# Output stage by seven block products, and an earlier attention schedule

## The chip, the cores and the metric

The kernel runs on one core of one Trainium2 chip. The time is the device time of one execution in microseconds (us). TensorE is the matmul engine, VectorE (DVE in the profile), ScalarE (ACT) and GpSimd (POOL) work element by element, and SyncE (SP) only issues DMAs. PSUM is where TensorE writes: eight banks of 512 fp32 numbers in each of 128 partitions. GpSimd doesn't read it here; it works on SBUF.

## The reference

Eight batches of 576 tokens with 8 heads of 64 go through a linear attention, and its output goes through a feed-forward network without a nonlinearity behind its product:

```python
q_p = phi(q, cos_w, sin_w)          # relu(q)*cos next to relu(q)*sin, 128 features
k_p = phi(k, cos_w, sin_w)
kv = np.einsum('bhsf,bhsd->bhfd', k_p, v)
z = np.sum(k_p, axis=2)
num = np.einsum('bhsf,bhfd->bhsd', q_p, kv)
den = np.einsum('bhsf,bhf->bhs', q_p, z)[..., None] + 1e-06
x = (num / den) laid out as [4608, 512]
a = x @ w1                          # [512, 1024]
b = x @ w2
out = ((a * b) @ w3) @ w_out        # w3 [1024, 1024], w_out [1024, 512]
```

## The kernel before

TensorE multiplies in bf16 and sums in fp32. The kernel first forms `w34b` = w3 @ w_out (1024 x 512) while tile 0 is at work, so that the network is two stages for each of nine tiles of 512 tokens:

- *Products*: for each of eight chunks `jc` of 128 hidden columns, four matmuls with w1 (`aT`) and four with w2 (`bT`), 512 wide (L432). ScalarE copies `aT` to `asb` (L469), VectorE multiplies `asb` with `bT` in PSUM to `abT[:, jc, :]` (L473).
- *Output*: for each of four blocks of 128 tokens, eight matmuls of `abT` with `w34b`, 512 wide (L486). ScalarE copies the sum to `osb` (L493). GpSimd issues the stores for tiles 0 to 7, two for a tile, at planned steps (L611); the last tile's go from SyncE, the last half block's from SyncE and ScalarE (L505).

The four PSUM tiles of these stages come from `ffn_tile` (L421): two pools of two buffers, so every tile reuses the bank of the fourth tile before it, and its first matmul waits for that tile's last reader. Two more banks hold `pnum`, a single buffer for attention, and two hold transposes.

`ffn_groups` is a generator. Each `yield` ends a step: a tile has 24, sixteen for the products (two for a `jc`) and eight for the output; tile 0 has 40. Tile t from 1 on begins at step 16+24t, so tile 2 at 64, tile 3 at 88, tile 8 at 208. All engines execute in the order in which the program emits their instructions; nothing is reordered. Between two steps the calls stand that `at(step, ...)` put there. Thus attention is woven into the feed-forward work:

- `plan_loads` issues the loads of k, v and q of a batch from GpSimd, each behind `hold_back` (L516): a one-element copy by ScalarE (`mark`) that GpSimd copies on (`seen`), so that the DMA is not issued before ScalarE has come so far.
- `prep_k` and `prep_q` make the features of one of five chunks: half by VectorE (L259), half by ScalarE (L263). From the fourth chunk of batch 1 on, queries are transposed by a DMA from SyncE (L277). `prep_v` copies values, from batch 2 on by GpSimd (L283).
- `kv_chunk` adds a chunk to the key-value products, eight 65-wide matmuls into `pnum` (L291). Behind the fifth, ScalarE and then VectorE copy them to `kvs` (L296, L297).
- `num` multiplies a chunk's queries with `kvs`, eight 65-wide matmuls into `pnum` (L349), and VectorE normalizes: three instructions, L359 to L361, to `xblk`.
- `x_tr` brings `xblk` into `xT`, the tile's input: in batches 0 and 1 by TensorE and a copy (L389), later by a DMA transpose from SyncE (L383).

`plan` gives the steps of these calls for a batch: `kf`, `qf` and `vc` for the features, `kv`, `nu` for `num`, `xt` for `x_tr` (as `nu` if left out). Batches 4 to 7 take theirs from `bases` (L598): a batch's first `num` is at its base.

Of the kernel before, what the change touches and what calls it, by code (L numbers as in the profile page):

```python
# [10 lines left out]
FP32 = mybir.dt.float32  # L11
BF16 = mybir.dt.bfloat16
I32 = mybir.dt.int32
ALU = mybir.AluOpType
ACTF = mybir.ActivationFunctionType

P = 128
# [51 lines left out]
def kernel(  # L69
# [11 lines left out]
    nc = tc.nc  # L81
# [4 lines left out]
    NT = T // 512  # L86

    const = ctx.enter_context(tc.tile_pool(name="const", bufs=1))
# [282 lines left out]
    def x_tr(b, c, by_vector=False):  # L371
        R, rows = ROWS[c], out_rows(b, c)
        xblk = att[b]["x"].pop(c)
        xf = xblk[:].rearrange("p g h d -> p (g h d)")
        if b % 2 == 0:
            slot = S * b + 128 * c
        else:
            slot = S * b + (0 if c == 4 else 64 + 128 * c)
        t, o = divmod(slot, 512)
        if t not in xT:  # L380
            xT[t] = xtp.tile([P, 4, 512], BF16, name="xT")
        if b >= 2 or (b == 1 and c == 3):
            nc.sync.dma_start_transpose(out=xT[t][:, :, ds(o, R)], in_=xf[rows])  # L383
            return
        pst = ps_tr.tile([P, 8, 128], BF16, name="pst")
        for kc in range(4):
            nc.tensor.transpose(pst[:, kc, :], xf[:, ts(kc, 128)], identb[:])
        copy = nc.vector.tensor_copy if by_vector else nc.scalar.copy
        copy(out=xT[t][:, :, ds(o, R)], in_=pst[:, 0:4, rows])  # L389
# [11 lines left out]
    def store(eng, osb, g, n, cols=slice(0, DM)):  # L401
# [13 lines left out]
        for i, rows in enumerate(parts):  # L415
            on = eng[i % 2] if isinstance(eng, tuple) else eng
            on.dma_start(out=rows[:, :, cols], in_=osb[64 * i:64 * i + rows.shape[0], :, cols])  # L417

    ffn_tiles = [0]

    def ffn_tile():  # L421
        pool = ps_ffn[ffn_tiles[0] // 2 % 2]
        ffn_tiles[0] += 1
        return pool.tile([P, 512], FP32, name="ffnps")

    def ffn_groups(t):
        x = xT[t]
        abT = fsb.tile([P, 8, 512], BF16, name="abT", bufs=2)

        def products(out, w, jc, tok):  # L430
            for kc in range(4):
                nc.tensor.matmul(out, lhsT=w[:, kc, ts(jc, 128)], rhs=x[:, kc, tok],  # L432
                                 start=(kc == 0), stop=(kc == 3))

        def on_half(half):

            for pair in range(2):
                a, b = ffn_tile(), ffn_tile()
                if pair == 0 and t == 0:
                    for quarter in range(2):  # L440
                        for i in range(2):
                            for ps, w in ((a, w1b), (b, w2b)):
                                products(ps[:, ds(256 * i + 128 * quarter, 128)], w, i,
                                         ds(256 * half + 128 * quarter, 128))
                            if half == 0 and quarter == 0 and i == 0:
                                yield
                        if quarter == 0:
                            yield
                else:
                    for ps, w in ((a, w1b), (b, w2b)):  # L450
                        for i in range(2):
                            products(ps[:, ts(i, 256)], w, 2 * pair + i, ts(half, 256))
                        if w is w1b and (t == 1 or half == 0):
                            yield
                asb = fsb.tile([P, 512], BF16, name="asb")
                nc.scalar.copy(out=asb[:], in_=a[:, :])
                nc.vector.tensor_mul(out=abT[:, ts(pair, 2), ts(half, 256)],
                                     in0=asb[:].rearrange("p (i n) -> p i n", i=2),
                                     in1=b[:, :].rearrange("p (i n) -> p i n", i=2))
                yield  # L460

        if t < 2:
            yield from on_half(0)
            yield from on_half(1)
        for jc in range(4 if t < 2 else 0, 8):
            aT = ffn_tile()
            products(aT[:, :], w1b, jc, slice(0, 512))
            asb = fsb.tile([P, 512], BF16, name="asb")
            nc.scalar.copy(out=asb[:], in_=aT[:, :])  # L469
            yield  # L470
            bT = ffn_tile()
            products(bT[:, :], w2b, jc, slice(0, 512))
            nc.vector.tensor_mul(out=abT[:, jc, :], in0=asb[:], in1=bT[:, :])  # L473
            yield
        if t == 0:
            for jp in range(8):
                for part in range(2):
                    w34_mm(jp, part)
                    yield
            early.close()  # L480
            holds.append(ctx.enter_context(tc.tile_pool(name="hold", bufs=HELD,
                                                        reuse_waits="tile")))
        for ms in range(3 if t == NT - 1 else 4):
            ops = ffn_tile()
            for jc in range(8):
                nc.tensor.matmul(ops[:, :], lhsT=abT[:, jc, ts(ms, 128)], rhs=w34b[:, jc, :],  # L486
                                 start=(jc == 0), stop=(jc == 7))
                if jc == 3:
                    yield
            if ms % 2 == 0:  # L490
                osb = holds[0].tile([P, 2, 512], FP32, name="osb")
                kept.append(osb)
            nc.scalar.copy(out=osb[:, ms % 2, :], in_=ops[:, :])  # L493
            if t == NT - 1:
                store(nc.sync, osb[:, ms % 2:ms % 2 + 1, :], 4 * t + ms, 1)
            yield
        if t == NT - 1:
            for half in range(2):
                cols = ts(half, 256)
                ops = ffn_tile()  # L500
                for jc in range(8):
                    nc.tensor.matmul(ops[:, 0:256], lhsT=abT[:, jc, ts(3, 128)],
                                     rhs=w34b[:, jc, cols], start=(jc == 0), stop=(jc == 7))
                nc.scalar.copy(out=osb[:, 1, cols], in_=ops[:, 0:256])
                store((nc.sync, nc.scalar), osb[:, 1:2, :], 4 * t + 3, 1, cols)  # L505
                yield


    HELD = 10
    holds, kept = [], []  # L510
    slots = [[] for _ in range(40 + 24 * (NT - 1))]

    def at(s, *calls):
        slots[s] += calls
# [8 lines left out]
    def plan(b, kf, vc, kv, qf, nu, loads=None, xt=None):  # L523
        order = order_of(b)
        for i, c in enumerate(order):
            at(kf[i], lambda c=c: prep_k(b, c))
            at(qf[i], lambda c=c: prep_q(b, c))
            at(vc[i], lambda c=c: prep_v(b, c))
        for i, c in enumerate(order):
            at(kv[i], lambda c=c, i=i: kv_chunk(b, c, i))  # L530
        for i, c in enumerate(order):
            at(nu[i], lambda c=c: num(b, c))
            at(xt[i] if xt else nu[i], lambda c=c: x_tr(b, c))

    def plan_loads(b, when):

        for piece, s in zip([(n, half) for n in "kqv" for half in range(2)], when):
            def issue(piece=piece):
                hold_back()
                load(b, *piece)  # L540
            at(s, issue)
# [42 lines left out]
    for jp, s in enumerate((13, 15, 17, 19, 21, 23, 25, 27)):  # L584
        at(s, lambda jp=jp: w3_tr(jp))

    plan(1, kf=(22, 23, 24, 25, 26), vc=(31, 31, 32, 32, 32), kv=(33, 33, 33, 34, 34),
         qf=(29, 30, 30, 31, 31), nu=(35, 37, 38, 40, 43), xt=(37, 38, 40, 42, 43))
    for c, s in zip(order_of(1), (31, 32, 34)):
        at(s, lambda c=c: q_tr(1, c))  # L590
    plan_loads(2, (27, 28, 31, 33, 35, 36))
    plan(2, kf=(33, 35, 37, 39, 40), vc=(41, 42, 43, 44, 45), kv=(45, 46, 46, 47, 47),
         qf=(40, 41, 42, 43, 44), nu=(48, 50, 52, 54, 57))
    plan_loads(3, (46, 49, 53, 55, 58, 61))
    plan(3, kf=(54, 57, 59, 61, 63), vc=(64, 65, 66, 67, 68), kv=(71, 72, 72, 73, 73),
         qf=(62, 64, 66, 69, 72), nu=(74, 77, 79, 84, 87))

    bases = [74, 101, 125, 151, 175]  # L598
    for b, last, base in zip(range(4, B), bases, bases[1:]):
        plan_loads(b, [last + s for s in (-8, -5, 1, 4, 8, 11)])  # L600
        plan(b, kf=[last + s for s in (4, 7, 10, 13, 15)],
             vc=[base + s for s in (-8, -7, -6, -5, -4)],
             kv=[base + s for s in (-3, -2, -2, -2, -1)],
             qf=[base + s for s in (-12, -9, -6, -3, 0)],
             nu=[base + s for s in (0, 2, 5, 8, 11)])

    for i in range(2 * (NT - 1)):
        def put(i=i):
            hold_back()
            store(nc.gpsimd, kept[i][:, :, :], 2 * i, 2)  # L610
        at((88, 115, 140, 166)[i] if i < 4 else 185 + 2 * (i - 4), put)  # L611

    g = 0
    for t in range(NT):
# [35 lines left out]
```

## Time and profile before

| what | us |
|---|---|
| median of 11 runs | 258.06 (255.86 to 260.5) |
| the profiled execution's own time | 256.24 |
| its span, first to last instruction | 254.1 |
| product stage, matmuls with w1 and w2 (L432), busy | 65.7 + 65.7 at 512 wide |
| output stage (L486), busy | 64.5 |
| VectorE's multiply (L473), 64 times | 43.8, 685 ns each |
| granted TensorE clock | 0.997 of full |

Busy times are sums over the span; engines overlap. A matmul's shown end is modelled and reaches over the start of the next one, so the time that a matmul takes of TensorE is read from start to start. Lines of groups give engine, operation, output and inputs, shapes, count, busy time, mean of one, and the idle time before them with what ended it. Lines in order of time give the start, the length and what was run. A stretch gives its length and then the busy time and number of instructions of PE, PEld (weight loads), DVE, ACT and POOL, the granted clock, the share of the DMA engines and GB/s.

### The profile page before, as it was taken

To read this page: it belongs to the slowest core of one execution; us is meant where nothing else is said; L and a number is where in the kernel's file an instruction comes from. 1 tells how busy PE (TensorE), PEld (TensorE's weight loads), DVE (VectorE), ACT (ScalarE), POOL (GpSimd) and SP (SyncE) were. 2 spreads that over 40 slices of the span, in tenths; PEclk is the share of its full clock that TensorE was granted. 3 is DMA by queue.
4 is the path that set the end of the run, shared out by engine and by line. 5 is a ranking of instruction groups with operands and counts; after the bars stand their busy time and mean duration, and the time that the engine had idled before them with its cause. 6 is when DMAs were issued, how large, how long until landed. Compare 5 with 4: busy or idle time off the path is not lost.

```text
span 254.1 us, 5038 instructions
## 1 busy us (share of the span) xinstructions
PE 243.2 (96%) x1867; PEld 130.9 (52%) x1867; DVE 138.3 (54%) x330; ACT 130.9 (51%) x270; POOL 93.7 (37%) x197
## 2 busy tenths in 40 slices
PE   8989999999799999999999999899999999999993
PEld 2578555575665445444544454345544544444442
DVE  6875654646768445646556755455477635303310
ACT  2775315677923783466446644564567333433322
POOL 7665230322242343125222712274126008885000
PEclk9999999999999999999999999999999999999998
DMA  6999999899999999999999999899999637998015
GB/s 194 183 194 202 209 204 204 103 138 155 150 162 122 173 145 155 137 130 206 131 156 143 205 133 183 117 181 148 194 135 185 108 72 147 336 294 259 0 41 124
DMA packets 83895, 41.02 MB, mean 161 GB/s; under 512 B 51488, under 2 KB 80416, under 8 KB 83872
## 3 DMA queue, kind: packets, MB, share of 16 engines
q0 software_dynamic: 35456, 27.20, 69.6%
q1 hardware_dynamic: 48256, 13.38, 35.0%
q8 instruction: 14, 0.23, 0.4%
q10 hardware_dynamic: 160, 0.13, 0.2%
q14 instruction: 9, 0.07, 0.1%
HBM read 38.80 MB, written 9.44 MB: 190 GB/s over the span
## 4 chain that ended last, share of the span: by engine, by line
PE 71%; DMA 16%; ACT 5%; DVE 3%; issue 2%; POOL 2%; ACTq 0%; POOLq 0%
PE ffnps L432 40%; PE ffnps L486 21%; DMA qs<-in_q_dram 7%; DMA w3b<-in_moe_w_dram 6%; PE pnum L349 3%; DMA w2b<-in_moe_w_dram 3%; PE ffnps L226 3%; PE pnum L291 3%; ACT qp L263 2%; DVE kvs L297 1%; ACT kvs L296 1%; PE pst L214 1%; ACT asb L469 1%; DVE xblk L361 1%; ACT w34b L229 0%
## 5 line engine op out<-in xcount | busy, mean ns | idle before, releaser
L432 PE MATMUL ffnps<-xT,w1b 128*128 128x512 bf16 (+2 forms) x336 | 75.0, 349 | 1.6 <-ACT osb L493 1.0
L432 PE MATMUL ffnps<-xT,w2b 128*128 128x512 bf16 (+2 forms) x336 | 75.0, 349 | 0.0
L473 DVE TENSOR_TENSOR abT<-asb,ffnps 128x512 bf16<-128x512 bf16 x64 | 43.8, 685 | 44.7 <-PE ffnps L432 41.9
L469 ACT CAST asb<-ffnps 128x512 bf16<-128x512 f32 x64 | 37.3, 584 | 55.4 <-PE ffnps L432 49.0
L486 PE MATMUL ffnps<-w34b,abT 128*128 128x512 bf16 x280 | 64.5, 379 | 0.0
L432 PEld LDWEIGHTS <-w1b 128*128 128x128 bf16 x336 | 30.7, 98 | 29.5 <-issue 2.3
L521 POOL COPY seen<-mark 1x1 bf16<-1x1 bf16 x52 | 9.6, 184 | 97.8 <-ACT mark L519 97.7
L432 PEld LDWEIGHTS <-w2b 128*128 128x128 bf16 x336 | 30.2, 98 | 25.8
L486 PEld LDWEIGHTS <-abT 128*128 128x128 bf16 x280 | 25.9, 98 | 28.0 <-DVE abT L473 0.2
L493 ACT COPY osb<-ffnps 128x512 f32<-128x512 f32 x35 | 20.5, 584 | 38.4 <-PE ffnps L486 38.3
L263 ACT ACTIVATE qp<-qs,sinv 128x512 bf16<-128x512 bf16 (+2 forms) x40 | 28.1, 716 | 1.6 <-DMA qs<-in_q_dram 1.6
L361 DVE TENSOR_TENSOR xblk<-pnum,den 128x512 bf16<-128x512 f32 (+1 forms) x39 | 26.9, 691 | 1.4
L263 ACT ACTIVATE kp<-ks,sinv 128x512 bf16<-128x512 bf16 (+1 forms) x35 | 25.0, 720 | 0.4 <-DMA ks<-in_k_dram 0.4
L417 POOL DMA_DIRECT2D out_dram<-osb x42 | 22.1, 532 | 3.8 <-issue 3.5
L283 POOL COPY va<-vs 128x512 bf16<-128x512 bf16 (+1 forms) x30 | 17.9, 628 | 13.0 <-DMA vs<-in_v_dram 10.5
L359 DVE TENSOR_SCALAR den<-pnum 128x8 f32<-128x8 f32 (+1 forms) x39 | 6.4, 163 | 26.5 <-PE pnum L349 26.3
L349 PEld LDWEIGHTS <-qpT 128*128 128x128 bf16 x320 | 15.1, 98 | 10.7 <-issue 4.1
L259 DVE TENSOR_SCALAR qp<-qs,cosv 128x512 bf16<-128x512 bf16 (+1 forms) x40 | 18.9, 482 | 2.0 <-DMA qs<-in_q_dram 2.0
L349 PE MATMUL pnum<-kvs,qpT 128*128 128x65 bf16 x312 | 16.4, 194 | 1.3 <-DVE kvs L297 1.2
L226 PE MATMUL ffnps<-woutb,w3T 128*128 128x512 bf16 x64 | 15.0, 379 | 0.0
L291 PEld LDWEIGHTS <-kp 128*128 128x128 bf16 x280 | 11.5, 98 | 5.4 <-PE ffnps L432 1.3
L291 PE MATMUL pnum<-va,kp 128*128 128x65 bf16 x280 | 12.2, 194 | 1.0 <-DVE xblk L361 1.0
(83 smaller groups left out, 181.6 us busy)
## 6 DMA issues: line engine op xcount, KB each, us to landing
out_dram<-osb POOLq DMA_DIRECT2D x16, 256.0 KB, 4.6
out_dram<-osb POOLq DMA_DIRECT2D x24, 128.0 KB, 4.0
qs<-in_q_dram POOLq DMA_DIRECT2D x9, 256.0 KB, 5.7
ks<-in_k_dram POOLq DMA_DIRECT2D x7, 320.0 KB, 6.4
qs<-in_q_dram POOLq DMA_DIRECT2D x7, 320.0 KB, 6.1
vs<-in_v_dram POOLq DMA_DIRECT2D x7, 320.0 KB, 5.3
ks<-in_k_dram POOLq DMA_DIRECT2D x7, 256.0 KB, 7.1
vs<-in_v_dram POOLq DMA_DIRECT2D x7, 256.0 KB, 4.9
```

The source lines that it names most:

```text
L226: nc.tensor.matmul(acc[:, :], lhsT=w3T[:, lc, :], rhs=woutb[:, lc, :], start=(lc == 0), stop=(lc == 7))
L259: nc.vector.tensor_scalar(out=dst[:R, c, :, 0:D], in0=src[:R, :, c, :], scalar1=0.0, scalar2=cosv[:R, at:at + 1], op0=ALU.max, op1=ALU.mult)
L263: nc.scalar.activation(out=dst[:R, c, 0:n, D:F], in_=src[:R, 0:n, c, :], func=ACTF.Relu, scale=sinv[:R, at:at + 1], bias=0.0)
L291: nc.tensor.matmul(kvt[:, h // 4, ds((h % 4) * 65, 65)], lhsT=kp[:, c, h, :], rhs=va[:, c, h, 0:D + 1], start=(i == 0 and h % 4 == 0), sto ...
L349: nc.tensor.matmul(nt[:, h // 4, ds((h % 4) * 65, 65)], lhsT=qpT[:, h, ds(at, 128)], rhs=kvs[:, h, :], start=True, stop=True)
L361: nc.vector.tensor_tensor(out=xblk[rows], in0=n4[:, :, :, 0:D], in1=den[rows].unsqueeze(3).to_broadcast([R, 2, 4, D]), op=ALU.mult)
L417: on.dma_start(out=rows[:, :, cols], in_=osb[64 * i:64 * i + rows.shape[0], :, cols])
L432: nc.tensor.matmul(out, lhsT=w[:, kc, ts(jc, 128)], rhs=x[:, kc, tok], start=(kc == 0), stop=(kc == 3))
L469: nc.scalar.copy(out=asb[:], in_=aT[:, :])
L473: nc.vector.tensor_mul(out=abT[:, jc, :], in0=asb[:], in1=bT[:, :])
L486: nc.tensor.matmul(ops[:, :], lhsT=abT[:, jc, ts(ms, 128)], rhs=w34b[:, jc, :], start=(jc == 0), stop=(jc == 7))
L493: nc.scalar.copy(out=osb[:, ms % 2, :], in_=ops[:, :])
```

## The change

The output of tiles 2 to 8 (`SEVEN = 2`) is computed by seven block products. For two token blocks of 128 (an a of two for each tile), the 256 x 1024 matrix A and the 1024 x 512 matrix `w34b` are cut in halves along each side; C's four blocks are sums of seven products of sums of blocks in place of eight products of blocks. Each of the seven is four matmuls, 256 wide: 28 for a pair, where sixteen 512-wide ones stood. The steps stay 24 a tile; the four of a pair hold products 3 and 6, 4 and 1, 5 and 2, and 7.

- `weight_sum` makes five sums of blocks of `w34b` once, on VectorE, at steps 66, 68, 70, 73 and 76 (1024 bf16 elements a partition each).
- `product_sums` makes the sums of A behind VectorE's multiply of `jc` 1, 3, 5, 6 and 7. For `jc` 1 and 3 it is one piece each of `asum6`, on GpSimd in tiles 2 to 6 (`BUSY = 7`), on VectorE in tiles 7 and 8; for 5, 6 and 7 four pieces each on VectorE, two of which overwrite `abT` blocks.
- `out_by_seven` allots four PSUM tiles for a pair: b3, b6, b4, b1. Products 5, 2 and 7 are added in PSUM onto b3, b4 and b1 after those were read once. Between the products, ScalarE copies to `osb`, and VectorE adds a PSUM tile to a part of `osb`. In tiles 2 to 6, two subtractions are done by GpSimd between parts of `osb`, and b6 is read after them at the pair's end. The last tile stores 256 columns of one block at a time from SyncE and ScalarE, eight pieces of two DMAs.

The schedule also moves: batches 4 to 7 have their bases 2, 2, 3 and 2 steps earlier, their value copies and key-value products one step further ahead of the base, and two value loads a step earlier; in batch 1, the last `num` and two `x_tr` are a step earlier and the copy of one `x_tr` goes from ScalarE to VectorE; batch 2 has its first key-value product and its query features a step later. Three planned stores move with the rest.

```diff
+    wsum = {i: const.tile([P, 4, 256], BF16, name=f"wsum{i}") for i in (1, 3, 4, 6, 7)}
+    asum = {i: const.tile([P, 4, 2, P], BF16, name=f"asum{i}") for i in (1, 5, 6)}
...
+    def product_sums(t, abT, lo, hi):
...
+        if lo < 4:
+            eng = nc.gpsimd if t < BUSY else nc.vector
+            eng.tensor_tensor(out=asum[6][:, n], in0=a21, in1=a11, op=ALU.subtract)
+            return
+        for out, in0, in1, op in ((asum[1][:, n], a11, a22, ALU.add),
+                                  (asum[5][:, n], a11, a12, ALU.add),
+                                  (a21, a21, a22, ALU.add), (a12, a12, a22, ALU.subtract)):
+            nc.vector.tensor_tensor(out=out, in0=in0, in1=in1, op=op)
...
+            b3, b6 = ffn_tile(), ffn_tile()
+            product(b3, 3, True)
+            nc.scalar.copy(out=c12, in_=b3[:, 0:256])
+            product(b6, 6, True)
+            yield
+            b4, b1 = ffn_tile(), ffn_tile()
+            product(b4, 4, True)
+            add(c11, c12, b4[:, 0:256])
+            product(b1, 1, True)
+            add(c22, c11, b1[:, 0:256])
+            yield
+            product(b3, 5, False)
+            nc.scalar.copy(out=c12, in_=b3[:, 0:256])
+            put(0, ts(1, 256))
+            product(b4, 2, False)
+            nc.scalar.copy(out=c21, in_=b4[:, 0:256])
+            put(1, ts(0, 256))
+            if t < BUSY:
+                add(c11, c11, c12, ALU.subtract, nc.gpsimd)
+                add(c22, c22, c21, ALU.subtract, nc.gpsimd)
+            else:
+                add(c11, c11, b3[:, 0:256], ALU.subtract)
+                add(c22, c22, b4[:, 0:256], ALU.subtract)
+                add(c22, c22, b6[:, 0:256])
+                put(1, ts(1, 256))
+            yield
+            product(b1, 7, False)
+            add(c11, c11, b1[:, 0:256])
+            put(0, ts(0, 256))
+            if t < BUSY:
+                add(c22, c22, b6[:, 0:256])
+            yield
...
             nc.vector.tensor_mul(out=abT[:, jc, :], in0=asb[:], in1=bT[:, :])
+            if by_seven(t) and jc in (1, 3, 5, 6, 7):
+                product_sums(t, abT, jc - (jc < 6), jc + 1)
...
-         qf=(29, 30, 30, 31, 31), nu=(35, 37, 38, 40, 43), xt=(37, 38, 40, 42, 43))
+         qf=(29, 30, 30, 31, 31), nu=(35, 37, 38, 40, 42), xt=(37, 38, 40, 41, 42))
...
-    plan(2, kf=(33, 35, 37, 39, 40), vc=(41, 42, 43, 44, 45), kv=(45, 46, 46, 47, 47),
-         qf=(40, 41, 42, 43, 44), nu=(48, 50, 52, 54, 57))
+    plan(2, kf=(33, 35, 37, 39, 40), vc=(41, 42, 43, 44, 45), kv=(46, 46, 46, 47, 47),
+         qf=(41, 42, 43, 44, 45), nu=(48, 50, 52, 54, 57))
...
-    bases = [74, 101, 125, 151, 175]
+    bases = [74, 99, 123, 148, 173]
...
-             kv=[base + s for s in (-3, -2, -2, -2, -1)],
+             kv=[base + s for s in (-4, -3, -3, -2, -2)],
```

More of the change, by code (lines that the diff above doesn't have):

```diff
@@ L417, in store, with w34_block, weight_sum @@
             on.dma_start(out=rows[:, :, cols], in_=osb[64 * i:64 * i + rows.shape[0], :, cols])
+    wsum = {i: const.tile([P, 4, 256], BF16, name=f"wsum{i}") for i in (1, 3, 4, 6, 7)}
+    asum = {i: const.tile([P, 4, 2, P], BF16, name=f"asum{i}") for i in (1, 5, 6)}
+    def w34_block(row, col):
+        return w34b[:, ts(row, 4), ts(col, 256)]
+    def weight_sum(i):
+        (r0, c0), (r1, c1), op = {1: ((0, 0), (1, 1), ALU.add), 3: ((0, 1), (1, 1), ALU.subtract),
+                                  4: ((1, 0), (0, 0), ALU.subtract), 6: ((0, 0), (0, 1), ALU.add),
+                                  7: ((1, 0), (1, 1), ALU.add)}[i]
+        nc.vector.tensor_tensor(out=wsum[i][:], in0=w34_block(r0, c0), in1=w34_block(r1, c1), op=op)
@@ new lines, in by_seven @@
+    def by_seven(t):
+        return t >= SEVEN
+    def product_sums(t, abT, lo, hi):
+        v = abT[:].rearrange("p j (a h n) -> p j a h n", a=2, h=2)
+        a11, a21 = (v[:, lo % 4:(hi - 1) % 4 + 1, :, h, :] for h in range(2))
+        a12, a22 = (v[:, 4 + lo % 4:4 + (hi - 1) % 4 + 1, :, h, :] for h in range(2))
+        n = slice(lo % 4, (hi - 1) % 4 + 1)
+        if lo < 4:
[6 more added lines that the diff above has]
+            nc.vector.tensor_tensor(out=out, in0=in0, in1=in1, op=op)
@@ new lines, in out_by_seven, with lhs, product, put @@
+    def out_by_seven(t, abT):
+        w = {1: wsum[1], 2: w34_block(0, 0), 3: wsum[3], 4: wsum[4], 5: w34_block(1, 1),
+             6: wsum[6], 7: wsum[7]}
+        for a in range(2):
+            def lhs(i, kc):
+                if i in (1, 5, 6):
+                    return asum[i][:, kc, a, :]
+                row, h = {2: (0, 1), 3: (0, 0), 4: (4, 1), 7: (4, 0)}[i]
+                return abT[:, row + kc, ts(2 * a + h, P)]
+            def product(ps, i, begin):
+                for kc in range(4):
+                    nc.tensor.matmul(ps[:, 0:256], lhsT=lhs(i, kc), rhs=w[i][:, kc, :],
+                                     start=(begin and kc == 0), stop=(kc == 3),
+                                     skip_group_check=True)
+            osb = holds[0].tile([P, 2, 512], FP32, name="osb")
+            kept.append(osb)
+            c11, c12 = osb[:, 0, 0:256], osb[:, 0, 256:512]
+            c21, c22 = osb[:, 1, 0:256], osb[:, 1, 256:512]
+            last = t == NT - 1
+            def put(h, cols):
+                if last:
+                    store((nc.sync, nc.scalar), osb[:, h:h + 1, :], 4 * t + 2 * a + h, 1, cols)
+            def add(out, in0, in1, op=ALU.add, eng=nc.vector):
+                eng.tensor_tensor(out=out, in0=in0, in1=in1, op=op)
+            b3, b6 = ffn_tile(), ffn_tile()
[30 more added lines that the diff above has]
+            yield
@@ L482, in ffn_groups @@
                                                         reuse_waits="tile")))
+        if by_seven(t):
+            yield from out_by_seven(t, abT)
+            return
         for ms in range(3 if t == NT - 1 else 4):
@@ L509 @@
     HELD = 10
+    SEVEN, BUSY = 2, 7
+    assert SEVEN > 1
     holds, kept = [], []
@@ L532, in plan @@
             at(nu[i], lambda c=c: num(b, c))
-            at(xt[i] if xt else nu[i], lambda c=c: x_tr(b, c))
+            at(xt[i] if xt else nu[i], lambda c=c: x_tr(b, c, by_vector=(b, c) == (1, 1)))
     def plan_loads(b, when):
@@ L596 @@
          qf=(62, 64, 66, 69, 72), nu=(74, 77, 79, 84, 87))
-    bases = [74, 101, 125, 151, 175]
+    bases = [74, 99, 123, 148, 173]
     for b, last, base in zip(range(4, B), bases, bases[1:]):
-        plan_loads(b, [last + s for s in (-8, -5, 1, 4, 8, 11)])
+        plan_loads(b, [last + s for s in (-8, -5, 1, 4, 7, 10)])
         plan(b, kf=[last + s for s in (4, 7, 10, 13, 15)],
-             vc=[base + s for s in (-8, -7, -6, -5, -4)],
-             kv=[base + s for s in (-3, -2, -2, -2, -1)],
+             vc=[base + s for s in (-9, -8, -7, -6, -5)],
+             kv=[base + s for s in (-4, -3, -3, -2, -2)],
              qf=[base + s for s in (-12, -9, -6, -3, 0)],
              nu=[base + s for s in (0, 2, 5, 8, 11)])
+    for i, s in zip((3, 6, 4, 1, 7), (66, 68, 70, 73, 76)):
+        at(s, lambda i=i: weight_sum(i))
     for i in range(2 * (NT - 1)):
@@ L610, in put @@
             store(nc.gpsimd, kept[i][:, :, :], 2 * i, 2)
-        at((88, 115, 140, 166)[i] if i < 4 else 185 + 2 * (i - 4), put)
+        at((88, 113, 137, 162)[i] if i < 4 else 185 + 2 * (i - 4), put)
     g = 0
```

## The prediction

> **What bounds the kernel now.** First the page's busy times and 40 slices: is there an engine that is full everywhere?
>
> ```profile
> PE 243.2 (96%) x1867; PEld 130.9 (52%) x1867; DVE 138.3 (54%) x330; ACT 130.9 (51%) x270; POOL 93.7 (37%) x197
> ...
> PE   8989999999799999999999999899999999999993
> ...
> DVE  6875654646768445646556755455477635303310
> ```
>
> TensorE is full from the fifth slice on, so work taken off it shortens the kernel until something makes it wait. VectorE's half is a mean; by tile (from the view of stretches, tiles 2 to 8, columns PE, PEld, DVE, ACT, POOL):
>
> ```profile
> 88.30:112.00 23.70, 23.64 (x177) 11.86 (x176) 11.56 (x27) 13.09 (x29) 8.20 (x18) 1.00 1.02 143
> 112.00:135.50 23.50, 23.20 (x174) 11.63 (x172) 14.22 (x34) 13.10 (x28) 8.12 (x18) 1.00 1.21 162
> ...
> 208.10:229.10 21.00, 21.00 (x106) 9.63 (x104) 7.53 (x14) 7.73 (x23) 16.36 (x39) 1.00 0.83 241
> 229.10:249.80 20.70, 20.70 (x104) 9.97 (x102) 5.50 (x8) 7.48 (x14) 3.34 (x8) 1.00 0.35 100
> ```
>
> Tiles 2 to 6 carry attention, 7 and 8 hardly any. Where TensorE does wait is in its order of time:
>
> ```profile
> 124.50 1.02 PE L432 MATMUL ffnps<-xT,w2b 128*128 128x512 bf16 x4
> 125.82 0.42 PE L349 MATMUL pnum<-kvs,qpT 128*128 128x65 bf16 x8 [0.30 <-DVE kvs L297]
> ...
> 157.49 1.89 PE L486 MATMUL ffnps<-w34b,abT 128*128 128x512 bf16 x8
> 160.37 1.02 PE L432 MATMUL ffnps<-xT,w1b 128*128 128x512 bf16 x4 [0.99 <-ACT osb L493]
> ...
> 67.92 1.04 PE L432 MATMUL ffnps<-xT,w2b 128*128 128x256 bf16 x8
> 70.00 0.42 PE L291 MATMUL pnum<-va,kp 128*128 128x65 bf16 x8 [1.04 <-DVE xblk L361]
> ```
>
> Shown ends include a drain of 0.16. From start to start, four 512-wide matmuls take 0.864 and eight 65-wide ones 0.255. The true stall at 125.82 is therefore 125.82-125.36 = 0.46 (alike at 149.55, 176.17 and 200.01), at 160.37 it is 1.15, at 70.00 1.2, and before a matmul at 67.05 0.53. The rows that price the rest:
>
> ```profile
> L473 DVE TENSOR_TENSOR abT<-asb,ffnps 128x512 bf16<-128x512 bf16 x64 | 43.8, 685 | 44.7 <-PE ffnps L432 41.9 <-ACT asb L469 2.5 <-issue 0.2
> L297 DVE CAST kvs<-pnum 128x260 bf16<-128x260 f32 x7 | 3.0, 429 | 8.0 <-ACT kvs L296 8.0
> L504 ACT COPY osb<-ffnps 128x256 f32<-128x256 f32 x2 | 0.7, 372 | 0.9 <-PE ffnps L502 0.9
> L502 PE MATMUL ffnps<-w34b,abT 128*128 128x256 bf16 x16 | 1.9, 273 | 0.0
> L417 SPq DMA_DIRECT2D out_dram<-osb x8: 466/552/589, 245.3 to 250.6; - x8
> ```
>
> VectorE's next instruction starts 0.08 before the shown end of the last, so one holds the engine 0.61 (multiply L473), 0.35 (260 elements from PSUM), 0.26 (key and query features), 1.03 (normalize, three instructions). A consumer starts 0.20 after the last matmul's issue slot; TensorE starts 0.05 after its releaser.
>
> **What the skill says.** The Trainium skill, "VectorE: DVE Perf Modes", tier table: a `tensor_tensor` runs two bf16 elements a cycle from SBUF and one with a PSUM operand; its errata section gives (N+151)/0.96 ns. The trace agrees for PSUM (512 elements: 691 ns in L361); no row shows two SBUF operands. "GPSIMD Engine Reference", section 3.1: about 2.6 cycles an element at 1.2 GHz for two inputs; here only one-input copies are seen (628 ns for 512). "SBUF — State Buffer", "Who interferes with whom": the two engines lock a shared port pair; the trace agrees, a 0.35 query feature takes 0.71 at 119.78 beside a GpSimd copy.
>
> **The change by parts.**
>
> *Matmuls.* A pair of 128-row blocks took 16 x 0.216 = 3.45 and takes 28 x 0.1094 = 3.06 (L502: 8 in 0.875); the 98 ns weight load still fits under each. That is 0.78 a tile, 4.7 for tiles 2 to 7.
>
> *Schedule.* Key-value products a step (0.86) ahead cover the four 0.46 stalls: 1.84. At 160.37 the x transposes of batch 5, issued at 153.7 with landings up to 6.2, are late; two steps (1.7) earlier clears 1.15. Tile 1's 0.53 and 1.2 come from the x copy behind four 0.62 query features on ScalarE and from the last normalize; copy by VectorE, x_tr and num a step earlier and kv of batch 2 at step 46 should clear most. Together 4.4. The moved loads carry their mark, GpSimd copy and issue along and keep 5 to 9 steps (over 4.3) between load and use; q and x transposes move with their producers on SP. I cost those at nothing: landings of 5 to 7 are mostly covered, and GpSimd has 15 idle a tile.
>
> *Added on VectorE* (occupancies): sums of bf16 at the page's rate, (256+151)/0.96 = 424, so 0.34 for 512 elements and 0.21 for 256; in a tile 4 x 0.34 + 8 x 0.21 = 3.0; adds with PSUM 8 x 0.34 = 2.8. Five weight sums of 0.61 in tile 2, four in idle time. VectorE goes to some 13+5.8 = 19 of 22.5: it fits on average. Its order doesn't. *GpSimd*: 256 fp32 with two inputs by the page 0.18+0.55 = 0.7; the `asum6` pieces 1.3, hidden eight steps ahead.
>
> *Order in tile 3* (clock 0 at jc=5's first matmul; batch 4 has num at its steps 11, 13, 16, 19, 22). The num at step 11 issues 1.73 to 1.98, but on VectorE its normalize stands behind multiply (1.93-2.53), four sums of jc 5 (to 3.91) and a query feature (4.17): it ends 5.2, visible 5.28. The single `pnum` buffer holds the num of step 13, due at 3.71, until 5.33: **stall 1.6**. Behind it on TensorE stand jc 7's products, done at 7.31. VectorE: multiply 6 and sums to 6.65, normalize to 7.68, multiply 7 to 8.28, sums to 9.12, feature 9.38. Products 3 and 6 need none of these and run to 8.18, num to 8.44, 4 to 8.87, 1 to 9.31, 5 to 9.75. Product 2 adds onto b4, which VectorE must have read: normalize first (to 10.41), then that add, visible 10.83: **stall 1.1**. Then product 7 to 11.76 and GpSimd's two subtractions, behind the copies of c12 and c21, to 12.63; VectorE's last add reads b6 till 13.1. The next pair's product 6 needs that bank and is due at 12.45, after a num: **stall 0.7**. The second pair's own product 2 is in time; its chain ends at 17.6, and the next tile's first w2b product, due 16.9 in the same bank, waits **0.75**. Sum 4.2 in tile 3.
>
> The same bookkeeping with the other step lists, clock at each tile's jc 5 (tile 2: at its first matmul). Tile 2 (num at 10, 13, 15, 20, 23): multiply 6 waits behind a weight sum to 15.7, sums to 16.55, the normalize of step 13 ends 17.58; the num of step 15 is due at 15.83: 1.87. Product 2 is due at 20.15, its bank read at 20.74: 0.65; b6 is read at 23.03, due 22.1: 0.98; the second product 2 again 0.65 behind a normalize; the next tile 0.28: 4.4. Tile 4 as 3: 4.2. Tile 5 (num 12, 14, 17, 20, 23): num due 5.09, held to 5.84, 0.75; multiply 7 then ends 8.86, product 4 waits 0.75; product 2 0.2, product 6 (due 11.67, read 12.57) 0.95, product 2 0.37, next tile 0.27: 3.3. Tile 6 (13, 15, 18, 21): kvs stands behind the sums, 0.42; num due 6.9, held to 7.65, 0.75; 0.35; product 6 (due 12.03, read 13.15, a normalize ahead in the queue) 1.17; next tile 0.5: 3.2. Together 19.3. Tile 7 subtracts on VectorE without attention, and its b6 is free in time: no stall.
>
> *Tile 8.* Its stores are 16 DMAs, half from ScalarE at 0.48 to 0.56 each. ScalarE's four issues of the first pair (2.2) delay the second pair's first copy to 5.8 after the stage's start; product 5 waits 0.9, and the last issue ends at about 9.5. Now it ends 250.87-242.73 = 8.14: +1.4, the 0.8 saved included.
>
> A wait of product 2 or 6 holds all that stands behind it on TensorE: the remaining products, the next num, the next tile. ScalarE loses nothing by it: three copies of 0.37 take the place of two of 0.58.
>
> **Sum**: -4.7-4.4+19.3+1.4 = +11.6. Span 254.1 to 265.7; the profiled execution 256.24 to 267.8. The median shown, 258.06, lies 1.8 above that execution, so about **269.5**.
>
> **Unknown costs.** Sums: at two a cycle taken, since bf16 features already run faster than one (345 for 512); at one a cycle each jc costs 0.5 to 1.1 more before a num, 1.6 a tile, +8. Below, no operand form excludes 0.25 for 512: -0.4 a tile. GpSimd's subtraction: lower end 0.41, the copy's (628-184)/512 x 256 + 184; two in a chain save 0.6 at ten places, with the sums -6 to -8; upper end 1.2 beside a lock, +4. Schedule: 0 to 4.7; if x stays late, 1.15 comes back.
>
> **Rivals.**
> 1. *Half the stalls* (chance 0.22): GpSimd near the copy rate and quicker sums leave about 10 of 19.3: 258.06+11.6-9.5 = 260. For: both prices are untested here. Against: the 0.61 multiply and the 1.03 normalize are measured, and alone fill 1.64 of a num's 1.73.
> 2. *Sums at one element a cycle* (0.15): 269.5+8 = 277.5. VectorE then needs 21 of each tile's time. Against: contiguous bf16 runs of 128.
> 3. *Faster* (0.12): one mechanism, the early release of PSUM. If the subtract chain gives b6 back within product 3 (0.44) and normalize leaves VectorE before the next num, stalls fall under 4: 258-4.7-4.4+1.4+4 = 254. It decides at 4.7+4.4-1.4 = 7.7 of stalls, 1.5 for each of five tiles. Against: b6's chain alone (copy 0.57, subtraction 0.7, add 0.42) is 1.7 behind product 2, and TensorE has 0.87 to give.
> That the matmuls don't get shorter I exclude: L502 shows the rate.
>
> **Chances.** The forecast 0.51 (its own range 264 to 275), rivals 0.22, 0.15, 0.12. Half a per cent (1.3) is about what a measurement tells. Faster: rival 3, 0.12; same: the low edge of rival 1, 0.05; slower 0.83. For 8 in 10 I reach from 257 (below: rival 3) to 278.5 (above: part of rival 2).
>
> **What would show it.** Out-stage matmuls 392 of 256 wide at 109 ns from start to start; TensorE busy near 238, but with idle before L349 put to xblk, before product 2 and product 6 put to VectorE's adds; tiles 2 to 6 near 24 to 27 each and tile 7 near 20.2; VectorE at 75%; the kv stalls and the one at 160 gone. It is wrong if the bf16 sums or GpSimd's subtractions come out far from 424 and 700 ns, or if TensorE's waits in tiles 2 to 6 sum to less than 8.

## The result: 7.4% slower

The median of 12 runs is 276.09 us (275.38 to 277.38), beside 257.75 for the kernel before in 47 runs: a ratio of 1.0743, with a 95% interval of 1.0716 to 1.0769. That is 18.3 more, where 11.6 was forecast. The profiled execution took 276.17 with a span of 274.2, so by spans the difference is 20.1. Below, the difference of each experiment is taken to the median of the kernel before as it ran beside it (257.9 to 258.2).

The page of the kernel after, busy times and the 40 slices of TensorE and VectorE:

```profile
PE 241.7 (88%) x2027; PEld 145.6 (53%) x2027; DVE 196.5 (72%) x488; ACT 130.2 (47%) x282; POOL 120.5 (44%) x227
...
PE   8789999999989997799779977998899879999972
...
DVE  6875735658764699577977797669789865774753
```

TensorE now has holes, one in each of tiles 2 to 6, and VectorE is nearly full in spots. The view of stretches shows tile 3, its middle from `jc` 5's multiply to the end of the last add before product 2, and the end from tile 8's output stage on (length, then busy time of PE, PEld, DVE, ACT, POOL):

```profile
116.52:143.71 27.19, 23.38 (x206) 14.19 (x202) 21.73 (x56) 13.98 (x33) 13.83 (x26) 1.00 1.00 139
128.87:138.47 9.60, 6.86 (x61) 4.31 (x58) 9.19 (x29) 2.96 (x8) 1.89 (x4) 1.00 1.36 144
260.02:274.20 14.18, 7.05 (x57) 5.28 (x55) 6.79 (x20) 2.24 (x6) 0.00 (x0) 0.99 0.33 75
```

Over the whole tile VectorE is busy 80%, but in its middle 9.19 of 9.60: there it is the bound. TensorE's order of time in tile 3, waiting lines only:

```profile
132.46 0.42 PE L349 MATMUL pnum<-kvs,qpT 128*128 128x65 bf16 x8 [1.71 <-DVE xblk L361]
...
138.07 0.60 PE L462 MATMUL ffnps<-w34b,abT 128*128 128x256 bf16 x4 [1.03 <-DVE osb L477]
...
140.62 0.60 PE L462 MATMUL ffnps<-wsum,asum 128*128 128x256 bf16 x4 [0.72 <-DVE osb L477]
...
145.41 1.02 PE L525 MATMUL ffnps<-xT,w2b 128*128 128x512 bf16 x4 [0.67 <-ACT asb L562]
```

These are the four places of the forecast: a `num` behind a normalize, product 2, the next pair's product 6, and the next tile's first w2b product. With 0.16 of drain each they are 1.87, 1.19, 0.88 and 0.83, against 1.6, 1.1, 0.7 and 0.75. The last is put down to ScalarE's copy, but VectorE's last read of b6 ended at 145.39 as well, and that is the bank the product needs. Behind the first stands this order on VectorE:

```profile
128.87 0.69 DVE L566 TENSOR_TENSOR abT<-asb,ffnps 128x512 bf16<-128x512 bf16 x1 [0.96 <-PE ffnps L525]
129.59 0.76 DVE L448 TENSOR_TENSOR asum<-abT 128x512 bf16<-128x512 bf16 x2
130.27 0.75 DVE L448 TENSOR_TENSOR abT<-abT 128x512 bf16<-128x512 bf16 x2
130.94 0.34 DVE L259 TENSOR_SCALAR qp<-qs,cosv 64x512 bf16<-64x512 bf16 x1
131.20 0.15 DVE L359 TENSOR_SCALAR den<-pnum 128x8 f32<-128x8 f32 x1
```

The normalize starts 2.33 after the multiply, because four sums and a feature lie between them. The sums follow each other at the 0.34 that was forecast, but the first starts 0.72 behind the multiply on whose output it depends, not 0.61.

### The profile page after: what moved, and what is told of

Same layout as the page of the kernel before. It is cut to its first block, busy times and chain, and to the rows that moved or that the text cites. A ratio compares the mean times of both kernels' runs of the same rounds, so it can differ in the third digit from the quotient of the medians.

```text
span 274.2 us, 5624 instructions
## 1 busy us (share of the span) xinstructions
PE 241.7 (88%) x2027; PEld 145.6 (53%) x2027; DVE 196.5 (72%) x488; ACT 130.2 (47%) x282; POOL 120.5 (44%) x227
## 5 line engine op out<-in xcount | busy, mean ns | idle before, releaser
L525 PEld LDWEIGHTS <-w1b 128*128 128x128 bf16 x336 | 30.5, 98 | 25.9 <-issue 0.6
L621 POOL COPY seen<-mark 1x1 bf16<-1x1 bf16 x52 | 10.3, 197 | 60.6 <-ACT mark L619 60.5
L477 DVE TENSOR_TENSOR osb<-osb,ffnps 128x256 f32<-128x256 f32 x64 | 26.2, 418 | 13.7 <-PE pnum L349 2.8
L477 POOL TENSOR_TENSOR osb<-osb 128x256 f32<-128x256 f32 x20 | 14.1, 727 | 30.0 <-DVE osb L477 23.8
L462 PEld LDWEIGHTS <-abT 128*128 128x128 bf16 x224 | 21.0, 97 | 11.2 <-issue 5.7
L259 DVE TENSOR_SCALAR qp<-qs,cosv 128x512 bf16<-128x512 bf16 (+1 forms) x40 | 24.4, 617 | 2.5 <-DMA qs<-in_q_dram 2.5
L462 PE MATMUL ffnps<-wsum,abT 128*128 128x256 bf16 x168 | 24.9, 272 | 0.6 <-DVE abT L566 0.6
L283 POOL COPY va<-vs 128x512 bf16<-128x512 bf16 (+1 forms) x30 | 19.0, 662 | 11.2 <-PE ffnps L525 9.4
L462 PE MATMUL ffnps<-wsum,asum 128*128 128x256 bf16 x112 | 16.8, 272 | 5.4 <-DVE osb L477 5.4
L462 PEld LDWEIGHTS <-asum 128*128 128x128 bf16 x168 | 16.3, 98 | 9.6 <-issue 7.9
L491 ACT COPY osb<-ffnps 128x256 f32<-128x256 f32 x14 | 5.2, 373 | 27.0 <-DVE osb L477 20.2
```

What stands on the lines that cost most here:

```text
L259: nc.vector.tensor_scalar(out=dst[:R, c, :, 0:D], in0=src[:R, :, c, :], scalar1=0.0, scalar2=cosv[:R, at:at + 1], op0=ALU.max, op1=ALU.mult)
L283: eng.tensor_copy(out=feat_of(b)[2][:R, c, :, 0:D], in_=raw[b, "v"][:R, :, c, :])
L462: nc.tensor.matmul(ps[:, 0:256], lhsT=lhs(i, kc), rhs=w[i][:, kc, :], start=(begin and kc == 0), stop=(kc == 3), skip_group_check=True)
L477: eng.tensor_tensor(out=out, in0=in0, in1=in1, op=op)
L621: nc.gpsimd.tensor_copy(out=seen[0:1, :], in_=mark[0:1, :])
```

## The experiments

Each edit is made to the kernel after. Lengths of tiles are read from the first w1 matmul of one to that of the next.

| kernel | median, us | to before | ratio (95%) |
|---|---|---|---|
| after | 276.09 | +18.3 | 1.074 (1.072 to 1.077) |
| e1: schedule alone | 255.16 | -3.1 | 0.988 (0.980 to 0.996) |
| e2: seven products, old schedule | 276.68 | +18.5 | 1.076 (1.065 to 1.086) |
| e3: b6 read early | 269.23 | +11.0 | 1.045 (1.036 to 1.054) |
| e4: sums a step later | 275.39 | +17.2 | 1.067 (1.059 to 1.076) |
| e5: no sums of A | 264.93 | +6.9 | 1.027 (1.021 to 1.032) |
| e6: tile 8 in eight | 273.71 | +15.7 | 1.064 (1.057 to 1.070) |
| e7: b6 early, half the sums on GpSimd | 275.86 | +17.9 | 1.070 (1.065 to 1.076) |
| e8: tile 7 alone in seven | 254.12 | -3.9 | 0.984 (0.980 to 0.988) |
| e9: no sums of A, b6 early | 257.95 | +0.1 | 0.997 (0.993 to 1.001) |
| e10: the products alone | 253.24 | -4.7 | 0.983 (0.976 to 0.990) |
| e11: b6 early, subtractions on VectorE | 270.45 | +12.6 | 1.049 (1.043 to 1.056) |
| e12: tiles 7 and 8 in seven | 253.90 | -4.2 | 0.988 (0.983 to 0.992) |

### The two halves of the change

e1 is the schedule without the products, e2 the products without the schedule:

```diff
-    SEVEN, BUSY = 2, 7
+    SEVEN, BUSY = 99, 7
...
-    for i, s in zip((3, 6, 4, 1, 7), (66, 68, 70, 73, 76)):
-        at(s, lambda i=i: weight_sum(i))
```

```diff
-    bases = [74, 99, 123, 148, 173]
+    bases = [74, 101, 125, 151, 175]
...
-             kv=[base + s for s in (-4, -3, -3, -2, -2)],
+             kv=[base + s for s in (-3, -2, -2, -2, -1)],
```

> The earlier schedule alone, with all tiles by eight block products as before. Theory A (the seven products cost the time, through single late instructions on VectorE and GpSimd for which TensorE stands still): the four kvs stalls of 0.46 and the 1.15 at tile 5's start are gone, tile 1 as it is in the changed kernel (no gain): 257.75 - 3 = about 254.8. Theory C (the moved steps cost the time, transposes of q and x come late): 264 or more.

> The seven products alone, with the schedule of before. Theory A: 276.1 + 3 = about 279. Theory C: 268 or less.

Alone, the schedule brings 3.1 (the interval is 0.4% to 2.0%): no wait for `kvs` is left, nor the one at tile 5, and tile 1 takes 25.15 instead of 26.28. Under the seven products it brings next to nothing: +18.5 without it (276.7, where 279 was expected), +18.3 with it. By tile it helps tile 1 (27.41 to 26.25) and tile 6 (27.39 to 25.70) and costs tiles 3 to 5 (26.26, 26.11, 26.48 to 27.19, 27.35, 27.36). So the moved steps are not the cause of the loss, but the schedule's gain doesn't carry over.

### b6 read early

```diff
             add(c22, c11, b1[:, 0:256])
+            add(c22, c22, b6[:, 0:256])
             yield
...
-            if t < BUSY:
-                add(c22, c22, b6[:, 0:256])
             yield
```

> The changed kernel with VectorE's add from b6 right behind its add from b1, so that b6's bank no longer waits for GpSimd's subtractions; as many instructions as before. Theory A (order): the waits before product 6 (seven, 6.5 with the drain) and before the next tile's first w2b product (five, 3.1) go: 276.1 - 8 = about 268. Theory B (VectorE is too full in tiles 2 to 6, 20 to 21 of 25 to 27, so that a wait taken away comes back at the next instruction): 273 or more.

One add moved in each pair, with no work less, takes 7.3 off (18.3 to 11.0). The waits before product 6 and before the next tile's w2b product are gone in tiles 2 to 6; those before `num` and product 2 stay, as this answer of waits of e3 shows (total, times, longest):

```profile
PE pnum L349 <- DVE xblk L361: 6.5, 5, 1.9
...
PE ffnps L462 <- DVE osb L477: 3.4, 5, 1.1
```

In the kernel after they were 6.7 and, with product 6's, 9.1 in 13 times. For b6 it was the order that cost: a bank ready behind product 6 was read only behind a chain of copies, subtractions and adds.

### The sums: later, or left out

e4 emits them behind the step's attention work; e5 leaves them out, and the products read blocks of `abT` in their place.

```diff
             nc.vector.tensor_mul(out=abT[:, jc, :], in0=asb[:], in1=bT[:, :])
+            yield
             if by_seven(t) and jc in (1, 3, 5, 6, 7):
                 product_sums(t, abT, jc - (jc < 6), jc + 1)
-            yield
```

```diff
             def lhs(i, kc):
-                if i in (1, 5, 6):
-                    return asum[i][:, kc, a, :]
-                row, h = {2: (0, 1), 3: (0, 0), 4: (4, 1), 7: (4, 0)}[i]
+                row, h = {1: (0, 0), 5: (0, 0), 6: (0, 1),
+                          2: (0, 1), 3: (0, 0), 4: (4, 1), 7: (4, 0)}[i]
...
-            if by_seven(t) and jc in (1, 3, 5, 6, 7):
-                product_sums(t, abT, jc - (jc < 6), jc + 1)
```

> The changed kernel with the sums of jc 5, 6 and 7 (and the asum6 pieces) emitted behind the step's attention calls, so that a normalize no longer stands behind them on VectorE. Theory A (order): the waits before num in tiles 2 to 6, 1.97, 1.71, 1.61, 0.77 and 0.66 as shown, go: 276.1 - 6.5 = about 269.5. Theory B (throughput of VectorE between jc 5 and the output stage, 7.4 of work in 5.7): the wait moves to product 4 and product 1, 273 or more.

> The changed kernel without the sums of A's blocks (VectorE's 3.0 a tile and GpSimd's two asum6 pieces are left out; the products read the blocks themselves), with all matmuls and all adds behind the products. Theory B (VectorE's work between jc 5 and the output stage is what makes num late): the waits before num and product 4 go, 9 to 10 in sum, those before products 2 and 6 stay: about 267. If the sums don't matter and the chain behind the products does all: 273 or more.

The later order doesn't help: the times of e4 and of the kernel after can't be told apart. In e4's tile 3 the wait before `num` fell, and products 4 and 2 waited in its place:

```profile
132.44 0.42 PE L349 MATMUL pnum<-kvs,qpT 128*128 128x65 bf16 x8 [0.25 <-DVE xblk L361]
...
136.72 0.28 PE L462 MATMUL ffnps<-wsum,abT 128*128 128x256 bf16 x1 [0.57 <-DVE abT L566]
...
139.15 0.60 PE L462 MATMUL ffnps<-w34b,abT 128*128 128x256 bf16 x4 [1.25 <-DVE osb L477]
```

Counted from the multiply of `jc` 5 (130.31 here, 128.87 in the kernel after), product 2 starts at 8.84, beside 9.20: of the 1.46 that the `num` waits less, 0.36 is left. Without the sums 11.4 goes (9 was expected). Sums are 4 x 0.34 + 8 x 0.21 = 3.0 a tile, 15.2 in tiles 2 to 6, and they lie in the stretch in which VectorE is full. In e5 one `num` of those tiles still waits for a normalize, and by little:

```profile
128.61 0.42 PE L349 MATMUL pnum<-kvs,qpT 128*128 128x65 bf16 x8 [0.25 <-DVE xblk L361]
```

The waits for VectorE's adds, before products 2 and 6 above all, stay (from the answer of waits of e5):

```profile
PE ffnps L460 <- DVE osb L475: 7.0, 11, 1.1
```

### Do the two add up?

> Without the sums of A's blocks (left out as in the run without sums) and with b6 read early. If the two causes are separate, their gains add: 276.1 - 11.2 - 6.9 = about 258. If they are one queue seen at two places, the second gives little: 262 or more.

e9 joins both edits (e3 and e5) and comes to the time of the kernel before: 11.4 + 7.3 = 18.7, measured 18.2. The two gains add within the noise, so they are separate causes. That the total comes out even is a balance, since the earlier schedule and the shorter matmuls should have put e9 below the kernel before. By tiles, 4, 6 and 7 take 23.29, 22.54 and 20.19, within 0.1 of e10 below, which has neither sums nor adds, and tile 5 takes 22.98, 0.5 more: there the two causes are nearly the whole loss. The rest is held back by other things. Tile 2 (25.70) ends with a wait for x that had not landed, tile 3 (25.02) had a granted clock of 0.93 in the view of stretches, and the last tile takes 27.3 with its 16 issues.

```profile
114.89 1.87 PE L521 MATMUL ffnps<-xT,w1b 128*128 128x512 bf16 x4 [1.93 <-DMA xT<-xblk]
```

### The products alone

e10 also leaves out every addition and subtraction behind the products; four ScalarE copies of 256 take their place in each pair.

```diff
             product(b6, 6, True)
+            nc.scalar.copy(out=c22, in_=b6[:, 0:256])
             yield
...
-            add(c11, c12, b4[:, 0:256])
             product(b1, 1, True)
-            add(c22, c11, b1[:, 0:256])
...
-            add(c11, c11, b1[:, 0:256])
+            nc.scalar.copy(out=c11, in_=b1[:, 0:256])
```

> The seven products with nothing else of the method: no sums and none of the adds and subtractions on VectorE and GpSimd (left out); each of a pair's four PSUM tiles is copied once by ScalarE, 256 wide. It bounds what the shorter matmuls are worth: 255.2 - 4.7 for tiles 2 to 7, and in tile 8 what the sixteen stores leave of 0.8: about 250. If 28 matmuls of 256 columns were not cheaper than 16 of 512 in place: 255.

Tiles 3, 5, 6 and 7 take 22.90, 22.48, 22.55 and 20.18, each 0.78 to 0.80 less than in e1: the saving as costed. The total missed its 250, because other tiles gave it back: the last takes 1.8 more than in e1, with its 16 issues, tile 1 takes 1.4 more, and tile 3's first matmul waits for x:

```profile
112.50 1.02 PE L509 MATMUL ffnps<-xT,w1b 128*128 128x512 bf16 x4 [0.72 <-DMA xT<-xblk]
```

### The last tile, and tile 7

```diff
     def by_seven(t):
-        return t >= SEVEN
+        return SEVEN <= t < NT - 1
```

> The changed kernel with tile 8 by eight products and its old stores. From the start of its first matmul to the end, tile 8 took 25.2 before and takes 28.0 now: 276.1 - 2.8 = about 273.3, if ScalarE's store issues between its copies (2.9 for three) are the cause. If the last tile's time is VectorE's sums: the same gain, but with the waits before product 4 in tile 8's trace, not before product 5.

The last tile in eight takes 2.6 off. In the kernel after, ScalarE issues three stores in its own order ahead of the copy that product 5's wait ends with:

```profile
263.88 2.88 ACTq L417 DMA_DIRECT2D out_dram<-osb  x3
266.88 0.37 ACT L481 COPY osb<-ffnps 128x256 f32<-128x256 f32 x1 [3.03 <-DMA out_dram<-osb]
```

```diff
-        return t >= SEVEN
+        return t == 7
```

> The schedule of the change, seven products in tile 7 alone (no attention but one num; b6 read early), all others in eight. If the matmuls saved are worth what was costed where VectorE has room: tile 7 20.2 in place of 21.0, 255.2 - 0.8 = about 254.4. If products by seven never pay: 255.2 or more.

e8 has seven products in tile 7 only, with b6 early: the tile takes 20.52 against 20.98 in e1. More than half the saving of 0.8 stays where almost no attention stands beside it.

### Work moved to another engine

Both have b6 early. e7 gives two of the four sums of A to GpSimd in tiles 2 to 6; e11 (`SEVEN, BUSY = 2, 2`) gives GpSimd's subtractions and `asum6` to VectorE.

```diff
+        other = nc.gpsimd if t < BUSY else nc.vector
...
-            nc.vector.tensor_tensor(out=out, in0=in0, in1=in1, op=op)
+            eng.tensor_tensor(out=out, in0=in0, in1=in1, op=op)
```

> Early b6 as in the run before, and in tiles 2 to 6 two of the four sums (asum5 and a12) by GpSimd. Theory B: 1.5 less of VectorE a tile takes about 1 off the wait before num and product 4 in each of five tiles: 269.2 - 4.5 = about 264.7. Rival D (the two engines' shared SBUF ports, or GpSimd's 1.16 for 512 elements behind its DMA issues, make the sums late): 269 or more, with waits before products 5 and 7.

> b6 read early, and VectorE in place of GpSimd in all tiles: asum6 (0.7 a tile) and the subtractions straight from PSUM (1.4 a tile). Theory B (VectorE's work is the bound in tiles 2 to 6): 2.1 more a tile of which about half falls into the full stretch, 269.2 + 4 to 8 = 273 to 277. If GpSimd's detour (copy, 0.73, add) is what still costs: 267 or less.

e7 is 6.9 worse than e3 although VectorE has two sums less. Part of that can be the granted clock, which the view of stretches gives as 0.94 in e7's tiles 2 and 4 and in e3's tile 2; but tiles 3, 5 and 6, at full clock in both, take 27.46, 28.56 and 25.00 beside 25.87, 26.74 and 24.08. In the order of time of e7's VectorE and of its GpSimd, the instructions of the two overlap, and VectorE's take longer:

```profile
129.81 0.42 DVE L450 TENSOR_TENSOR asum<-abT 128x512 bf16<-128x512 bf16 x1
130.16 1.37 DVE L450 TENSOR_TENSOR abT<-abT 128x512 bf16<-128x512 bf16 x1
131.45 1.23 DVE L259 TENSOR_SCALAR qp<-qs,cosv 64x512 bf16<-64x512 bf16 x1
```

```profile
129.86 1.39 POOL L450 TENSOR_TENSOR asum<-abT 128x512 bf16<-128x512 bf16 x1 [1.91 <-DVE abT L566]
131.33 1.21 POOL L450 TENSOR_TENSOR abT<-abT 128x512 bf16<-128x512 bf16 x1
```

A sum of 0.42 takes 1.37, and a feature of 0.34 takes 1.23. This agrees with the Trainium skill, "SBUF — State Buffer", section "Who interferes with whom", which says that a VectorE instruction with two SBUF inputs contends with a GpSimd instruction that reads SBUF, and that a feature's kind (`tensor_scalar`) can contend too. The expected place was missed: the extra wait is before `num` (12.2 in all, 6.5 in e3), not before products 5 and 7. e11 lies between both expectations, 1.6 above e3 with intervals that overlap: VectorE has more to do and the chain is shorter, and the run doesn't part the two. Without GpSimd's two-input work in tiles 2 to 6 the waits before `num` are still 6.7 in five places, beside 6.5 in e3, so that work is not what makes `num` late.

### A version that beats both

e12 keeps seven products in tiles 7 and 8 only, b6 early, with tile 8's stores 512 wide, seven from SyncE and one from ScalarE.

```diff
-    SEVEN, BUSY = 2, 7
+    SEVEN, BUSY = 7, 7
...
-                put(1, ts(1, 256))
+                put(1, slice(0, 512))
...
-            put(0, ts(0, 256))
+            put(0, slice(0, 512))
```

> Seven products in tiles 7 and 8 alone, b6 read early, and tile 8's stores 512 columns wide: eight DMAs, seven from SyncE and one from ScalarE behind its last copy. If the store issues between ScalarE's copies made tile 8 late, it now takes at most the 25.2 of the version by eight, perhaps 24.8: 254.1 - 0.4 = about 253.7. If the adds behind the products or their latency made it late: 255.5 or more, with TensorE waiting before product 5 or 6 in tile 8.

It is faster than before by 1.25% (0.8 to 1.7), as e8 is by 1.6% (1.2 to 2.0); the runs don't tell the two apart, nor either from e1. The last tile missed its expectation: 25.99 beside 25.19 in e1. No product 5 or 6 waits there, but the stores come at the end: SyncE's seven issues take 4.91 from 243.38 on. Most of the gain in both is the schedule's; what shows of the seven products is tile 7, 20.5 in both beside 20.98 in e1.

## Why the prediction was right in its mechanism and short in its size

The direction, the places and most prices held. The measured 276.1 lies just above the forecast's own range of 264 to 275 and inside the wider one of 257 to 278.5. By the total alone it is nearer to rival 2 (277.5) than to 269.5; what excludes rival 2 is the price of a sum, below. The forecast by tile, made from the prediction's own terms with each wait of a "next tile" put into the tile where it falls, against the spans from tile to tile:

| tile | before | forecast | after | miss |
|---|---|---|---|---|
| 1 | 26.28 | 24.9 | 26.25 | +1.4 |
| 2 | 23.66 | 27.0 | 27.93 | +0.9 |
| 3 | 23.48 | 26.0 | 27.19 | +1.2 |
| 4 | 24.89 | 26.7 | 27.35 | +0.7 |
| 5 | 23.83 | 26.4 | 27.36 | +1.0 |
| 6 | 23.75 | 25.5 | 25.70 | +0.2 |
| 7 | 20.97 | 20.7 | 22.07 | +1.4 |
| 8 to the end | 25.22 | 26.6 | 28.03 | +1.4 |

With 0.3 ahead of tile 1 the misses sum to 8.5, and 11.6 + 8.5 is the 20.1 of the spans.

- **Matmuls: right.** The pair's 28 are 0.1094 apart; e10 shows 0.79 a tile, 0.78 forecast.
- **Prices: right.** The open ones came out near the values taken, so rivals 1 and 2 fall. From the groups by form and the page:

```profile
L448 DVE TENSOR_TENSOR asum<-abT 128x512 bf16<-128x512 bf16 x14 | 5.3, 422 | 0.2
L448 DVE TENSOR_TENSOR asum<-abT 128x256 bf16<-128x256 bf16 x28 | 6.9, 288 | 0.5
```

```profile
L477 POOL TENSOR_TENSOR osb<-osb 128x256 f32<-128x256 f32 x20 | 14.1, 727 | 30.0 <-DVE osb L477 23.8
```

  The sums of 512 take 422 ns (the prediction's estimate from the Trainium skill, "VectorE: DVE Perf Modes", tier table and errata section: 424), those of 256 take 288; GpSimd's subtraction 727 (0.7 taken), and its `asum6` piece 1161 (1.3 taken).
- **"VectorE's next instruction starts 0.08 before the shown end of the last": failed for dependent instructions.** The multiply and its first sum are 0.72 apart, not 0.61, in `jc` 5 to 7; the second add of a pair of dependent ones is 0.2 late (0.94 for two, 0.75 for two independent ones). That is 0.1 to 0.2 for each such step in a chain; in tile 3 the stalls came out 0.1 to 0.3 longer than forecast, and smaller gaps stand beside them that no term had.
- **"ScalarE loses nothing by it": failed, but at hardly any cost that the trace shows.** Its second copy into c12 waits for VectorE's add, which still reads c12; the copies of c21 and of the next group stand behind it. In the answer of waits it is 20.2 in ten places:

```profile
ACT osb L491 <- DVE osb L477: 20.2, 10, 3.0
```

  That is ScalarE's time and not TensorE's. In tile 3 the copy ends at 138.48 and GpSimd's first subtraction starts at 138.69, but it also needs VectorE's second add, which ends at 138.55. Of the ten starts of GpSimd's two subtractions the trace puts nine to VectorE and one to this copy.
- **"Tile 7 ... its b6 is free in time: no stall": failed.** The wait at its start is 0.58 (0.5 forecast), and behind it stand gaps of 0.18, 0.26, 0.09 and 0.21 and a wait of 0.57 before product 6. In e8, with b6 early, product 6 follows without a wait.
- **"Five weight sums of 0.61 in tile 2": mis-sized in one of them.** Four took a shown 0.7 each; one took 2.21 beside GpSimd's work. The multiply, a feature (1.46, beside GpSimd's copies) and `kvs` came late behind it, and a `num` waited 0.73 with the drain, which no term had and which is most of tile 2's miss:

```profile
94.90 2.21 DVE L430 TENSOR_TENSOR wsum<-w34b 128x1024 bf16<-128x1024 bf16 x1
...
100.08 0.42 PE L349 MATMUL pnum<-kvs,qpT 128*128 128x65 bf16 x8 [0.57 <-DVE kvs L297]
```

- **Tile 8, "+1.4": mis-sized, +2.8.** ScalarE's four issues of the first pair hold it for 3.4 (0.56 and the 2.88 above), where 2.2 was taken. Product 5 waits 1.2 (0.9 forecast), and products 6 and 2 wait 0.97 and 0.23, which the sum did not have.
- **Schedule, "Together 4.4": mis-sized.** Alone it is 3.1; under the seven products 0.2. In e1 the four `kvs` stalls and tile 5's are gone as forecast. Under the seven products that time is waited for elsewhere: in tile 3 the longest wait before `num` is 0.77 with the old schedule (e2) and 1.71 with the earlier one. Tile 1's 1.4 is there in e1 (1.1) and not in this execution, where two `num` waited 0.46 and 0.29 for transposed queries. That is not a single case. With the earlier schedule, tile 1 took 25.2 to 25.4 in the three kernels that keep tiles 2 to 6 in eight products (e1, e8, e12), and 25.9 to 28.3 in the nine others, although its own steps are the same; why stays open.
- **"It fits on average. Its order doesn't": half right.** For b6 it was the order (e3). For `num` and product 2 it was VectorE's load within ten microseconds: leaving the sums out takes them in tile 3 from 1.71 to 0.25 and from 1.03 to 0.24 (e5), and the one other order that was tried moves them (e4).
- **Rival 3** fell on the point named for it: stalls stayed far above 1.5 a tile.

## What to carry to other kernels

Price work that is added to a side engine within the stretch where it falls, between the instructions that bring it work and the ones that wait for it; a mean over a tile (80% here) hides that it is the bound for a third of it. Read a PSUM bank when it is ready and not where the formula ends: one add moved was worth 7.3. Gains need not add: the schedule's 3.1 alone was 0.2 in front of a late engine, while the two causes of the loss, taken away together, did add.

## What the runs showed of the hardware

- A VectorE instruction that reads the output of the one before it starts after its full length and 0.03 more (0.72 for a multiply of 0.69), or 0.10 more between fp32 adds (0.52 for 0.42); independent ones start 0.08 before that end (0.34 for sums of 0.42).
- GpSimd's work stretches VectorE's instructions on SBUF: in e7, VectorE's 512-element sums into `abT` take 1.37 in tiles 2 to 6, where GpSimd's sums run beside them, and 0.42 in tiles 7 and 8, where none do. Its copies can do as much: in the kernel after, a feature at 124.75 took 1.91 beside three of them.
- GpSimd took 727 ns for two inputs of 256 fp32 and 1161 for 512 bf16.
- A DMA issue held ScalarE 0.48 to 0.56 in the kernel before and 0.50 to 1.33 in the kernel after, and its next copy waits for it as for any other work.
